# Retention and a routed two-layer network on one core: slots decoded in 16 bits, and what the first gather waits for

## The chip, the core and the metric

The kernel runs on one core of a Trainium2 chip. A core has TensorE (PE; its weight loads have a row of their own, PEld), VectorE (DVE), ScalarE (ACT) and GpSimd (POOL), each with an instruction stream of its own, and queues for DMA: here SyncE's queue writes and loads with plain DMAs, and GpSimd's queue issues the indirect ones (gathers and scatters by row numbers). The metric is device time in microseconds (us) of one execution.

## The reference, cut to what matters

```python
def _attn_ref(q, k, v):                      # (4, 8, 768, 64): batch, heads, steps, width
    for t in range(S):
        state = gamma * state + k_t outer v_t      # gamma differs by head
        y[:, :, t] = scale * (q_t @ state)

def _moe_ref(x, w_gate, w1, w2):             # x: (3072, 512), 8 experts, w1 512 x 1024, w2 1024 x 512
    cap = N // E                             # 384 tokens for each expert
    order = np.argsort(-(x @ w_gate).flatten())
    for idx in order:                        # greedy: the highest (token, expert) pair first
        tok, e = idx // E, idx % E
        if assigned[tok] >= 0 or counts[e] >= cap: continue
        assigned[tok] = e; counts[e] += 1
    for e in range(E):
        out[assigned == e] = np.maximum(x[assigned == e] @ w1[e], 0) @ w2[e]
```

The retention is computed in chunks of 128 steps, and its rows, transposed to one row for each token, are the x of the second part. All are float32; the kernel makes the large products of the network from high and low halves (three matmuls for one).

## The kernel before, in words

**First part (to about 92 us).** 24 units (4 batches by 6 chunks of 128 steps) run through TensorE; VectorE masks the scores, ScalarE copies out. For the rows of x, 17 units are turned on VectorE in 32 by 32 blocks (`block_rows`) and written by the SyncE queue to a DRAM tile `xs`. The last 7 units are turned on TensorE (`row_part`, four transposes for each unit, two to a half), copied by ScalarE to a tile `xr` (`row_out`, a pool of `ROWBUFS` buffers) and written to `xs`. Beside this the gate's logits L are made, and a search for the threshold of the first expert begins.

**Search and decode (`search(n)`, n = 0 to 7 in the order in which experts fill).** The tokens are laid out as 128 partitions by 24 columns. A threshold is found in two counts on TensorE (`count_pairs`), then `Wq` marks the 384 chosen tokens. Two matmuls give each of them its rank; `s0` is 32 plus the rank, or 0. The decode then makes a list of token numbers by slot: `high_slots` splits s0 into `low` (five bits) and `hi`, compares hi with the numbers 0 to 11 (`A`), multiplies by the partition number and by the column number (`V`); `low_slots` compares low with 0 to 31 (`ob`, two tiles); `places` multiplies ob and V on TensorE, six matmuls of 4 columns each; `tokens_of_slots` sums this by four selector matmuls and two VectorE instructions to `idx`. All these small VectorE instructions are called through one helper and stand as L154 in the profile. `bad` collects checks (a group of chosen tokens that isn't 384, and the like); if it is set at the end, a slow exact path (`settle`, after the `If`) runs instead. All the small TensorE results of the search share one PSUM buffer, `psm`.

**The change of part.** The first search is run by hand: `STEPS` says how many halves of rows are turned after each of its steps, and `FILL` how many idle matmuls (`hot<-zer`, 512 columns) TensorE does after the second threshold and after the ranks. The first weights `wraw` are gathered as soon as the expert's code is known (`fetch_w`, L952), then three gathers of x by `idx` (`fetch_x`, L985), then 23 idle matmuls (`HOT`) are run, and the gathered rows `xg` are turned on TensorE (`pt`, L998), copied by ScalarE (`xh`, L1003, behind the first two quarters of the weight split `w1h`, L971) and multiplied (`by_thirds`, L1027).

**Network (to 402 us).** For each expert `mm1` (L1048, `ph`) and `mm2` (L1070, `py`) run on TensorE, with ReLU and splits on ScalarE and VectorE. A planner with rough costs puts the instructions of later searches, weight splits, turns of x and gathers between the matmuls; the order is fixed when the kernel is built.

Of the kernel before, what the change touches and what calls it, by code (L numbers as in the profile page):

```python
# [52 lines left out]
SEND = 10  # L53
STEPS = 7, 1, 2
HOT = 23
WAIT = 3
THIRDS = 2
FILL = (2, 7)
READY0 = 0
# [5 lines left out]
def tile_retention_moe(ctx: ExitStack, tc: tile.TileContext, qkv, wg, w1, w2,  # L65
# [47 lines left out]
    def constants():  # L113
        for t, x in [(onesb, 1.0), (un, 1.0)] + [(t, 0.0) for t in (zer512, Sc, Wq, bad, *sgs)]:
            nc.gpsimd.memset(t, x)
        nc.gpsimd.affine_select(ub, onesb, pattern=[[1, 128]], compare_op=OP.is_gt, fill=0.0, base=0,
                                channel_multiplier=-1)
        nc.gpsimd.affine_select(ident, onesb, pattern=[[1, 128]], compare_op=OP.is_equal, fill=0.0, base=0,
                                channel_multiplier=-1)
        nc.gpsimd.iota(iot, pattern=[[1, 64]], base=0, channel_multiplier=0, allow_small_or_imprecise_dtypes=True)  # L120

    def selectors():
        nc.vector.tensor_reduce(quad, ident.rearrange("p (q r) -> p q r", q=4), axis=AX.X, op=OP.max)
        yield
        nc.vector.tensor_reduce(rowq, ident.rearrange("p (q r) -> p r q", q=4), axis=AX.X, op=OP.max)
        for q in range(4):
            yield
            nc.vector.tensor_scalar(selq[:, q], rowq[:, None, :].to_broadcast([128, 4, 32]), quad[:, q:q + 1], None,
                                    op0=OP.mult)
# [228 lines left out]
    def scores(us):  # L358

        c = units[us[0]][1]  # L360
        for u in us:
            if u == B + 1:
                gate(0)
            k_, q_ = LD[u][:, 0], LD[u][:, 1]
            sc = [bank() for _ in range(2)]
            for pr in range(HP):
                for s in range(2):
                    r, w = slice(64 * s, 64 * s + 64), slice(pr * C, pr * C + C)
                    nc.tensor.matmul(sc[s][:, pr, :], k_[r, w], q_[r, w], start=True, stop=True)  # L369
            am = rw.tile([128, 2, HP, C], F32, name="am", bufs=4)  # L370
            for s in range(2):
                masked.append(nc.vector.tensor_tensor(am[:, s], sc[s], dm[:, s], op=OP.mult))  # L372
            qs = ks = None
            if c:
                qs = rw.tile([128, HP, C], F32, name="qs", bufs=4)
                nc.gpsimd.tensor_tensor(qs, q_.rearrange("p (a b) -> p a b", a=HP), qtb, op=OP.mult)
# [60 lines left out]
    def row_part(pr_, i, d0, d1):  # L437
        b, c = units[i]
        for d in range(d0, d1):
            nc.tensor.transpose(pr_[:, 128 * d:128 * d + 128], YS[b, c][:, d, :], ident)  # L440

    def row_out(pr_, i):
# [8 lines left out]
        t0 = (b * NC + c) * 128  # L451
        nc.sync.dma_start(xs[t0:t0 + 128, :], xr)

# [14 lines left out]
    def send(b, c0, x):  # L468

        xv = xs.rearrange("(b n k) (g x) -> b g k n x", b=B, k=32, g=4)  # L470
        for g in range(4):
            nc.sync.dma_start(xv[b, g ^ 2 * (b % 2), :, 4 * c0:4 * c0 + x.shape[1]], x[32 * g:32 * g + 32])

# [7 lines left out]

    written = []

# [198 lines left out]
    def high_slots(s0, o, n, eng=None):  # L682

        hi = sw.tile([128, COLS], I32, name="hi")
        ve.tensor_scalar(hi, s0, 5, None, op0=OP.arith_shift_right)
        low = sw.tile([128, COLS], I32, name="low")
        ve.tensor_scalar(low, s0, 31, None, op0=OP.bitwise_and)
        A = sw.tile([128, COLS, NB], BF, name="A")
        tt(A, bc(hi, NB), cb(iot[:, o:o + NB], NB), OP.is_equal)
        V = sw.tile([128, COLS, 2, NB], BF, name="V")  # L690
        if eng is None:
            ve.tensor_scalar(V[:, :, 0], A, c_("pcol"), None, op0=OP.mult)
        else:
            eng.activation(V[:, :, 0], A, AF.Copy, scale=c_("pcol"))
        tt(V[:, :, 1], A, bc(tokc, NB), OP.mult)
        return V, low

    def low_slots(low):

        ob = []  # L700
        for c0, c1 in ((0, OBS), (OBS, COLS)):
            ob.append(sw.tile([128, c1 - c0, 32], BF, name=f"ob{c0}"))
            tt(ob[-1], bc(low[:, c0:c1], 32), cb(iot[:, 0:32], 32, c1 - c0), OP.is_equal)
        return ob
# [8 lines left out]
    def places(V, ob, eng=None):  # L713
        pl = ps_small([128, 4, 2 * NB])
        for k in range(COLS // 4):
            c = 4 * k
            o = ob[c // OBS][:, c % OBS:c % OBS + 4]
            te.matmul(flat(pl), flat(o), V[:, c:c + 4].rearrange("p c a n -> p (c a n)"), start=(k == 0),
                      stop=(k == COLS // 4 - 1))
        pls = sw.tile([128, 4, 2 * NB], BF, name="pls")  # L720
# [32 lines left out]
    def search(n):  # L753
# [62 lines left out]
        te.matmul(rk, onesb, Sc[:, 0:COLS + 1], start=False, stop=True)  # L816
        s0 = sw.tile([128, COLS], I32, name="s0")
        ve.scalar_tensor_tensor(s0, rk[:, 0:COLS], 32.0, Wq[:, 0:COLS], op0=OP.add, op1=OP.mult)
        if not last:
            ve.scalar_tensor_tensor(bad, rk[:, COLS:], float(CAP), bad, op0=OP.not_equal, op1=OP.max)  # L820
        if n == 0:
# [33 lines left out]
    def settle(n):  # L855
# [511 lines left out]
```

## Time and profile before

| | |
|---|---|
| runs shown | 404.22, 405.19, 406.41 us (median 405.19) |
| profiled execution | 404.51 us; span of its instructions 402.8 us; granted clock of TensorE 0.997 |
| busy over the span | PE 388.0 us (96%), PEld 337.8 (84%), DVE 274.6 (68%), ACT 156.6 (39%), POOL 147.0 (36%) |
| chain that ended last | PE 61%, DVE 16%, issue 14%, POOL 3%, ACT 2%, DMA 2% |
| DMA | 77.50 MB, mean 192 GB/s |

A row of the chain names the work that the end waited for at that moment. The names are those of the program's tiles without numbers: `V<-A,tokc` writes V from A and tokc. "Idle before" is the time in which the engine did nothing ahead of an instruction, with what ended it behind the arrow; "issue" means that the profile shows nothing that it waited for.

### The profile page before, as it was taken

How to read it: one execution, taken by the hardware profiler on the slowest of the kernel's cores; microseconds unless marked ns; L12 is line 12 of the kernel's file. 1: busy time of each engine (PE TensorE's matmuls, PEld its weight loads, DVE VectorE, ACT ScalarE, POOL GpSimd, SP SyncE). 2: the span in 40 equal slices, each digit the busy share in tenths (PEclk: the TensorE clock that was granted, in tenths of full speed). 3: DMA queues.
4: the chain of work that ended last, by engine and by line, in shares of the span. 5: the costliest groups of instructions: out<-in, count | busy, mean ns of one | idle time of the engine just before them, and what ended most of it. 6: DMA issues, size and time to landing. Idle time of an engine off the chain costs nothing.

```text
span 402.8 us, 8473 instructions
## 1 busy us (share of the span) xinstructions
PE 388.0 (96%) x3457; PEld 337.8 (84%) x3459; DVE 274.6 (68%) x640; ACT 156.6 (39%) x285; POOL 147.0 (36%) x163
## 2 busy tenths in 40 slices
PE   8999999997999999999989999999999999999993
PEld 5998999973798889879868987898799889889982
DVE  5359779878899489859848894897688157156300
ACT  1422434342571264157216524343454165157210
POOL 5488783202611620441261341352255138021011
PEclk9999999999999999999999999999999999999998
DMA  7999998887643762382384383266147316710001
GB/s 284 421 416 421 404 324 247 204 224 244 213 175 104 206 253 55 127 302 105 106 251 192 132 282 137 66 231 253 54 156 244 148 46 181 323 54 26 2 26 60
DMA packets 22825, 77.50 MB, mean 192 GB/s; under 512 B 2678, under 2 KB 11640, under 8 KB 16122
## 3 DMA queue, kind: packets, MB, share of 16 engines
q0 software_dynamic: 8448, 46.14, 32.7%
q1 hardware_dynamic: 14330, 30.74, 21.5%
q8 instruction: 29, 0.48, 0.5%
q14 instruction: 18, 0.14, 0.1%
HBM read 64.29 MB, written 12.58 MB: 191 GB/s over the span
## 4 chain that ended last, share of the span: by engine, by line
PE 61%; DVE 16%; issue 14%; POOL 3%; ACT 2%; DMA 2%; another core or an unknown queue 1%; SPq 0%; POOLq 0%; ACTq 0%; DVEq 0%
PE py L1070 24%; PE ph L1048 20%; PE yp L414 4%; PE sc L369 4%; DVE am L372 3%; PE pt L998 2%; PE psm L154 2%; DVE w1l L154 2%; DMA ld<-qkv 2%; PE TP L429 1%; DVE cmp L154 1%; POOL out L1082 1%; PE sc L501 1%; PE yp L399 1%; PE py L711 1%
## 5 line engine op out<-in xcount | busy, mean ns | idle before, releaser
L1048 PE MATMUL ph<-xh,w1h 128*128 128x384 f32 x248 | 81.9, 343 | 0.1
L1048 PE MATMUL ph<-xlo,w1h 128*128 128x384 f32 x256 | 81.7, 335 | 0.2 <-DVE xlo L154 0.2
L1048 PE MATMUL ph<-xh,w1l 128*128 128x384 f32 x256 | 81.5, 335 | 0.0
L1070 PE MATMUL py<-w2h,hh 128*128 128x512 f32 x192 | 78.4, 408 | 0.0
L1070 PE MATMUL py<-w2l,hh 128*128 128x512 f32 x192 | 75.2, 392 | 0.0
L1070 PE MATMUL py<-w2h,hl 128*128 128x512 f32 x192 | 75.1, 391 | 0.0
L1082 POOL DMA_INDIRECT out<-yo,oix x24 | 28.0, 1165 | 115.2 <-ACT yo L1080 103.7
L952 POOL DMA_INDIRECT wraw<-w,wix x32 | 38.8, 1213 | 60.5 <-DVE un L154 46.9
L1053 ACT ACTIVATE hh<-ph 128x384 fp32r<-128x384 f32 x64 | 31.4, 490 | 61.7 <-PE ph L1048 57.4
L154 DVE TENSOR_TENSOR w1l<-wraw,w1h 128x1024 fp32r<-128x1024 f32 (+1 forms) x36 | 39.3, 1102 | 15.5 <-ACT w1h L971 15.3
L1048 PEld LDWEIGHTS ph<-xlo,w1h 128*128 128x128 f32 x256 | 47.7, 188 | 0.5 <-DVE xlo L154 0.5
L1048 PEld LDWEIGHTS ph<-xh,w1h 128*128 128x128 f32 x248 | 46.4, 188 | 1.6 <-DVE hl L154 0.6
L1048 PEld LDWEIGHTS ph<-xh,w1l 128*128 128x128 f32 x256 | 47.7, 188 | 0.0
L154 DVE SCALAR_TENSOR_TENSOR hl<-ph,hh 128x384 fp32r<-128x384 f32 x64 | 34.5, 553 | 16.0 <-ACT hh L1053 15.4
L985 POOL DMA_INDIRECT xg<-xs,idx x24 | 29.0, 1209 | 42.6 <-issue 27.7
L1070 PEld LDWEIGHTS py<-w2h,hl 128*128 128x128 f32 x192 | 36.1, 188 | 7.8
L372 DVE TENSOR_TENSOR am<-sc,dm 128x512 f32<-128x512 f32 x48 | 30.0, 681 | 17.5 <-PE sc L369 17.5
L1070 PEld LDWEIGHTS py<-w2l,hh 128*128 128x128 f32 x192 | 36.2, 188 | 6.5 <-DVE w2l L154 0.7
L1070 PEld LDWEIGHTS py<-w2h,hh 128*128 128x128 f32 x192 | 36.1, 188 | 5.8
L154 DVE TENSOR_TENSOR w2l<-wraw,w2h 128x1024 fp32r<-128x1024 f32 x32 | 38.6, 1219 | 2.3 <-ACT w2h L971 1.6
L971 ACT ACTIVATE w1h<-wraw 128x1024 fp32r<-128x1024 f32 (+1 forms) x36 | 33.7, 958 | 7.8 <-issue 6.7
L1080 ACT ACTIVATE yo<-py 128x512 f32<-128x512 f32 x23 | 13.8, 598 | 58.6 <-PE py L1070 43.4
(178 smaller groups left out, 544.8 us busy)
## 6 DMA issues: line engine op xcount, KB each, us to landing
ld<-qkv SPq DMA_DIRECT2D x20, 1024.0 KB, 12.2
xs<-x SPq DMA_DIRECT2D x32, 128.0 KB, 3.0
ld<-qkv SPq DMA_DIRECT2D x4, 768.0 KB, 5.4
xs<-xr SPq DMA_DIRECT2D x7, 256.0 KB, 2.1
wraw<-w,wix POOLq DMA_INDIRECT x32
xg<-xs,idx POOLq DMA_INDIRECT x24
out<-yo,oix POOLq DMA_INDIRECT x24
xs<-x SPq DMA_DIRECT2D x4, 64.0 KB, 1.8
```

What stands on the lines that cost most here:

```text
L154: return f(o, *a, **k)
L369: nc.tensor.matmul(sc[s][:, pr, :], k_[r, w], q_[r, w], start=True, stop=True)
L372: masked.append(nc.vector.tensor_tensor(am[:, s], sc[s], dm[:, s], op=OP.mult))
L414: nc.tensor.matmul(yp[o:o + 64, pr, :], values(u)[:, 2 * pr + s, :], st[u][0][:, s, pr, :], start=(not c and pr == 0), stop=(pr == HP - 1) ...
L952: nc.gpsimd.indirect_dma_start(out=t, out_offset=None, in_=w1v if nm == "w1" else w2v, in_offset=bass.IndirectOffsetOnAxis(ap=wix[:, hf:hf ...
L971: nc.scalar.activation(p[0], p[2], AF.Copy)
L985: nc.gpsimd.indirect_dma_start(out=t, out_offset=None, in_=xs, in_offset=bass.IndirectOffsetOnAxis(ap=found[n][0][:, j:j + 1], axis=0))
L1048: nc.tensor.matmul(ph, a[:, o:o + 128], x_[:, d], start=(k == 0 and not begun), stop=(k == len(prods) - 1), skip_group_check=begun)
L1053: nc.scalar.activation(hh[:, f], ph, AF.Relu)
L1070: nc.tensor.matmul(py, h_[:, f, t], a[:, o:o + DM], start=(k == 0), stop=(k == 23))
L1080: nc.scalar.activation(yo, py, AF.Copy)
L1082: sct = nc.gpsimd.indirect_dma_start(out=out, out_offset=bass.IndirectOffsetOnAxis(ap=oix[:, j:j + 1], axis=0), in_=yo, in_offset=None, bo ...
```

## The change

It has four parts.

1. **Decode in 16 bits.** `s0`, `low` and `hi` become int16, and the number tables they are compared with become bfloat16 tables made at the start on GpSimd (`iolow`, 128 elements, `iohigh`, 312). `low` is taken first and `hi` is `s0 - low`, so hi now waits for low. A, V and ob are laid out with the tokens' columns innermost. So V is now read by the slot matmuls with a step of 24 elements, and the selectors `selq` of the last sum are built from another table (`four`, one VectorE reduction more).
2. **Checks behind the token numbers (first search only).** The check of the ranks goes from in front of `low` to behind `ob`; the other two (three instructions) go behind `idx`. In the later searches the checks stay where they were.
3. **First gather.** A GpSimd memset (`early`) waits for everything that wrote or read `xs` and the buffers (the list `gone`); the first gather of x behind it waits for VectorE alone.
4. **Rows in one go.** `STEPS` 7, 1, 2 becomes 9, 1, 0; `FILL` 2, 7 becomes 5, 7; `ROWBUFS` 4 becomes 5.

```diff
-ROWBUFS = 4
+ROWBUFS = 5
-STEPS = 7, 1, 2
+STEPS = 9, 1, 0
-FILL = (2, 7)
+FILL = (5, 7)
+    iolow = sw.tile([128, 32, 4], BF, name="iolow")
+    iohigh = sw.tile([128, NB + 1, COLS], BF, name="iohigh")
...
+        for t, k in ((iolow, 1), (iohigh, 32)):
+            nc.gpsimd.iota(t, pattern=[[k, t.shape[1]], [0, t.shape[2]]], base=0, channel_multiplier=0,
+                           allow_small_or_imprecise_dtypes=True)
...
+        nc.vector.tensor_reduce(four, ident.rearrange("p (j r) -> p r j", r=4), axis=AX.X, op=OP.max)
...
-        hi = sw.tile([128, COLS], I32, name="hi")
-        ve.tensor_scalar(hi, s0, 5, None, op0=OP.arith_shift_right)
-        low = sw.tile([128, COLS], I32, name="low")
+        low = sw.tile([128, COLS], I16, name="low")
         ve.tensor_scalar(low, s0, 31, None, op0=OP.bitwise_and)
-        A = sw.tile([128, COLS, NB], BF, name="A")
-        tt(A, bc(hi, NB), cb(iot[:, o:o + NB], NB), OP.is_equal)
-        V = sw.tile([128, COLS, 2, NB], BF, name="V")
+        hi = sw.tile([128, COLS], I16, name="hi")
+        tt(hi, s0, low, OP.subtract)
+        A = sw.tile([128, NB, COLS], BF, name="A")
+        tt(A, hi[:, None, :].to_broadcast([128, NB, COLS]), iohigh[:, o:o + NB], OP.is_equal)
+        V = sw.tile([128, 2, NB, COLS], BF, name="V")
...
-            ob.append(sw.tile([128, c1 - c0, 32], BF, name=f"ob{c0}"))
-            tt(ob[-1], bc(low[:, c0:c1], 32), cb(iot[:, 0:32], 32, c1 - c0), OP.is_equal)
+            k = (c1 - c0) // 4
+            ob.append(sw.tile([128, k, 32, 4], BF, name=f"ob{c0}"))
+            tt(ob[-1], low[:, c0:c1].rearrange("p (k r) -> p k r", r=4)[:, :, None, :].to_broadcast([128, k, 32, 4]),
+               iolow[:, None].to_broadcast([128, k, 32, 4]), OP.is_equal)
...
-            o = ob[c // OBS][:, c % OBS:c % OBS + 4]
-            te.matmul(flat(pl), flat(o), V[:, c:c + 4].rearrange("p c a n -> p (c a n)"), start=(k == 0),
-                      stop=(k == COLS // 4 - 1))
+            o = ob[c // OBS][:, c % OBS // 4]
+            te.matmul(flat(pl), flat(o), V[:, :, :, c:c + 4].rearrange("p a n c -> p c (a n)"),
+                      start=(k == 0), stop=(k == COLS // 4 - 1))
...
-        if not last:
+        def full_rows():
             ve.scalar_tensor_tensor(bad, rk[:, COLS:], float(CAP), bad, op0=OP.not_equal, op1=OP.max)
+        if n and not last:
+            full_rows()
...
         ob = low_slots(low)
-        if not last:
-            ve.scalar_tensor_tensor(bad, both, code, bad, op0=OP.not_equal, op1=OP.max)
-            alone(oh, unf if n else None)
+        if n == 0:
+            full_rows()
+        elif not last:
+            one_left()
...
         idx = tokens_of_slots(pls)
+        if n == 0:
+            one_left()
...
+    early = nc.gpsimd.memset(spacer, 0.0)
+    for o_ in gone:
+        tc.add_manual_dep(early.ins, o_.ins.name, ...)
     side.finish(0)
```

How the order of instructions changes, at three places. The line numbers differ by the lines that the change adds (L154 is now L162, L952 is L978, L985 is L1011).

VectorE, the first decode, before (from the ranks to the copy of the slot sums):

```order
L154 SCALAR_TENSOR_TENSOR s_1679<-psm,Wq 128x24
L154 SCALAR_TENSOR_TENSOR bad<-psm,bad 128x1
L154 TENSOR_SCALAR hi<-s_1679 128x24
L154 TENSOR_SCALAR low<-s_1679 128x24
L154 TENSOR_TENSOR A<-hi,iot 128x288
L154 TENSOR_TENSOR V<-A,tokc 128x24x12
L154 TENSOR_TENSOR ob_1699<-low,iot 128x384
L154 TENSOR_TENSOR ob_1701<-low,iot 128x384
L154 SCALAR_TENSOR_TENSOR bad<-both,code,bad 128x1
L154 TENSOR_REDUCE et<-oh 128x1
L154 SCALAR_TENSOR_TENSOR bad<-et,bad 128x1
L154 CAST pls<-psm 128x96
```

The same stretch now:

```order
L162 SCALAR_TENSOR_TENSOR s_1689<-psm,Wq 128x24
L162 TENSOR_SCALAR low<-s_1689 128x24
L162 TENSOR_TENSOR hi<-s_1689,low 128x24
L162 TENSOR_TENSOR A<-hi,iohigh 128x288
L162 TENSOR_TENSOR V<-A,tokc 128x288
L162 TENSOR_TENSOR ob_1708<-low,iolow 128x384
L162 TENSOR_TENSOR ob_1710<-low,iolow 128x384
L162 SCALAR_TENSOR_TENSOR bad<-psm,bad 128x1
L162 CAST pls<-psm 128x96
L162 TENSOR_TENSOR own<-psm,quad 128x24
L162 TENSOR_REDUCE idx<-own 128x3
L162 SCALAR_TENSOR_TENSOR bad<-both,code,bad 128x1
```

The check that reads the ranks' PSUM (`bad<-psm,bad`) went from the second place to behind ob; the other three checks are now behind idx; hi stands behind low.

GpSimd, from the first gather of weights on, with what each instruction waits for, before:

```order
L952 DMA wraw_95<-w,wix 128x2048 [waits DVE_49]
L985 DMA xg<-xs,idx 128x512 [waits DMAHW3_49,DMAHW2_49,DMAHW4_49,DMAHW1_49,DMAHW5_49,DMAHW0_49,DMAHW6_49,DVE_49,DMAHW7_49,PE_49,Pool_49]
L985 DMA xg<-xs,idx 128x512 x2
L952 DMA wraw<-w,wix 128x2048
L1156 COPY spacer<-xh 1x1 [waits Activation_49]
```

And now:

```order
L978 DMA wraw_98<-w,wix 128x2048 [waits DVE_49]
L1152 MEMSET spacer 1x1 [waits DMAHW3_49,DMAHW4_49,DMAHW2_49,DMAHW5_49,DMAHW1_49,DMAHW6_49,DMAHW0_49,DMAHW7_49,PE_49,Pool_49]
L1011 DMA xg<-xs,idx 128x512 [waits DVE_49]
L1011 DMA xg<-xs,idx 128x512 x2
L978 DMA wraw<-w,wix 128x2048
L1186 COPY spacer<-xh 1x1 [waits Activation_49,Pool_49]
```

Of the eleven waits of the first gather of x, ten went to the memset ahead of it, and VectorE's stayed.

TensorE, the first slot matmuls, with their waits, before:

```order
L711 MATMUL py<-zer,onesb 128x512
L154 LDWEIGHTS ob_1699 [waits PE_49,DVE_49]
L154 MATMUL psm<-V,ob_1699 128x96 [waits Activation_49]
L154 LDWEIGHTS ob_1699
L154 MATMUL psm<-V,ob_1699 128x96
L154 LDWEIGHTS ob_1699
L154 MATMUL psm<-V,ob_1699 128x96
L154 LDWEIGHTS ob_1701 [waits DVE_49]
L154 MATMUL psm<-V,ob_1701 128x96
```

And now:

```order
L726 MATMUL py<-zer,onesb 128x512
L162 LDWEIGHTS ob_1708 [waits PE_49,DVE_49]
L162 MATMUL psm<-V,ob_1708 128x96 [waits Activation_49]
L162 LDWEIGHTS ob_1708
L162 MATMUL psm<-V,ob_1708 128x96
L162 LDWEIGHTS ob_1708
L162 MATMUL psm<-V,ob_1708 128x96
L162 LDWEIGHTS ob_1710
L162 MATMUL psm<-V,ob_1710 128x96
```

Before, the second tile of ob had a wait for VectorE of its own. Now the first weight load's wait covers it: the sums go to the one psm buffer, which the check behind the second ob has to have read.

## Rows read from the trace of the kernel before

**Rows 1.** Windows. Columns: stretch, length, busy of each engine (instructions), clock, DMA share.
```profile
104.00:357.00 253.00, 250.10 (x1496) 220.09 (x1497) 181.97 (x431) 106.90 (x175) 86.49 (x92) 1.00 0.49 172
```

**Rows 2.** The chain of waits, 86 to 113 us. Columns: start us, us, engine and line.
```profile
95.29 0.94 DVE ob L154 x2
...
97.29 4.99 PE py L711 x23
...
103.44 0.60 ACT xh L1003
```

**Rows 3.** Timeline of VectorE. Columns: start us, us, line, operation, out<-in, shapes, idle.
```profile
93.56 0.13 DVE L154 SCALAR_TENSOR_TENSOR wix<-code,cs 128x2 int32<-128x2 f32 x1
...
93.91 0.18 DVE L154 SCALAR_TENSOR_TENSOR s<-psm,Wq 128x24 int32<-128x24 f32 x1
94.01 0.15 DVE L154 SCALAR_TENSOR_TENSOR bad<-psm,bad 128x1 f32<-128x1 f32 x1
94.13 0.18 DVE L154 TENSOR_SCALAR hi<-s 128x24 int32<-128x24 int32 x1
...
94.34 0.46 DVE L154 TENSOR_TENSOR A<-hi,iot 128x288 bf16<-128x288 int32 x1
94.83 0.46 DVE L154 TENSOR_TENSOR V<-A,tokc 128x288 bf16<-128x288 bf16 x1
95.21 1.02 DVE L154 TENSOR_TENSOR ob<-low,iot 128x384 bf16<-128x384 int32 x2
...
96.74 0.25 DVE L154 CAST pls<-psm 128x96 bf16<-128x96 f32 x1
...
97.54 0.19 DVE L154 TENSOR_REDUCE idx<-own 128x3 int32<-128x24 f32 x1
...
99.68 0.26 DVE L154 TENSOR_TENSOR eqc<-oh,codeo 128x192 bf16<-128x192 bf16 x1
```

**Rows 4.** Timeline of GpSimd, the first gathers.
```profile
93.99 1.16 POOL L952 DMA_INDIRECT wraw<-w,wix  x1 [20.18 <-DVE un L154]
98.58 1.11 POOL L985 DMA_INDIRECT xg<-xs,idx  x1 [3.43 <-DVE lim L154]
```

**Rows 5.** Timeline of ScalarE around the first gathers.
```profile
93.39 0.66 ACT L448 ACTIVATE xr<-py 128x256 f32<-128x256 f32 x2 [0.93 <-PE py L440]
...
102.11 1.15 ACT L971 ACTIVATE w1h<-wraw 128x512 fp32r<-128x512 f32 x2 [6.74 <-issue]
```

**Rows 6.** Timeline of TensorE, the count of pairs.
```profile
91.19 0.31 PE L154 MATMUL psm<-oh,cmp 128*128 128x16 bf16 x6 [0.56 <-DVE cmp L154]
```

**Rows 7.** DMA issues of the page. Columns: out<-in, queue, KB each, median us to landing.
```profile
xs<-xr SPq DMA_DIRECT2D x7, 256.0 KB, 2.1
```

**Rows 8.** Timeline of TensorE, the first rows of x.
```profile
102.70 0.66 PE L998 MATMUL pt<-ident,xg 128*128 128x128 f32 x4 [0.43 <-DMA xg<-xs,idx]
```

**Rows 9.** Timeline of GpSimd at the start.
```profile
3.96 0.40 POOL L120 IOTA iot<- 128x64 f32 x1
6.41 1.04 POOL L379 TENSOR_TENSOR ld<-ld,ktb 128x512 f32<-128x512 f32 x1 [2.06 <-DMA ktb<-ktab]
```

**Rows 10.** The chain of waits over the whole span, two later decodes.
```profile
192.71 0.47 DVE A L154
...
193.86 0.94 DVE ob L154 x2
...
290.60 0.66 DVE V L154 x2
```

**Rows 11.** Timeline of TensorE, the slot matmuls of a later decode.
```profile
163.45 0.43 PE L154 MATMUL psm<-V,ob 128*128 128x96 bf16 x6
```

**Rows 12.** Waits of TensorE, 110 to 357 us. Columns: waiter <- releaser: us, times, longest.
```profile
PE psm L154 <- DVE sg L154: 2.0, 1, 2.0
...
PE ph L1048 <- DVE xlo L154: 0.2, 1, 0.2
```

**Rows 13.** Timeline of ScalarE, a late count.
```profile
210.17 0.17 ACT L220 ACTIVATE ng<-psm 64x8 f32<-64x8 f32 x1 [5.08 <-remote]
```

More of the change, by code (lines that the diff above doesn't have):

```diff
@@ L11 @@
 I32 = mybir.dt.int32
+I16 = mybir.dt.int16
 U32 = mybir.dt.uint32
@@ L102, in tile_retention_moe @@
     quad = sw.tile([128, 4], F32, name="quad")
+    four = sw.tile([128, 4], F32, name="four")
     rowq = sw.tile([128, 32], F32, name="rowq")
@@ L120, in constants @@
         nc.gpsimd.iota(iot, pattern=[[1, 64]], base=0, channel_multiplier=0, allow_small_or_imprecise_dtypes=True)
+        for t, k in ((iolow, 1), (iohigh, 32)):
+            nc.gpsimd.iota(t, pattern=[[k, t.shape[1]], [0, t.shape[2]]], base=0, channel_multiplier=0,
+                           allow_small_or_imprecise_dtypes=True)
     def selectors():
         nc.vector.tensor_reduce(quad, ident.rearrange("p (q r) -> p q r", q=4), axis=AX.X, op=OP.max)
+        nc.vector.tensor_reduce(four, ident.rearrange("p (j r) -> p r j", r=4), axis=AX.X, op=OP.max)
         yield
-        nc.vector.tensor_reduce(rowq, ident.rearrange("p (q r) -> p r q", q=4), axis=AX.X, op=OP.max)
+        nc.vector.tensor_reduce(rowq, ident.rearrange("p (j r) -> p j r", r=4), axis=AX.X, op=OP.max)
         for q in range(4):
             yield
-            nc.vector.tensor_scalar(selq[:, q], rowq[:, None, :].to_broadcast([128, 4, 32]), quad[:, q:q + 1], None,
+            nc.vector.tensor_scalar(selq[:, q], rowq[:, None, :].to_broadcast([128, 4, 32]), four[:, q:q + 1], None,
                                     op0=OP.mult)
@@ L375, in scores @@
                 qs = rw.tile([128, HP, C], F32, name="qs", bufs=4)
-                nc.gpsimd.tensor_tensor(qs, q_.rearrange("p (a b) -> p a b", a=HP), qtb, op=OP.mult)
+                scaled = nc.gpsimd.tensor_tensor(qs, q_.rearrange("p (a b) -> p a b", a=HP), qtb, op=OP.mult)
+                if u == nu - 1:
+                    gone.append(scaled)
             if c < NC - 1:
@@ L439, in row_part @@
         for d in range(d0, d1):
-            nc.tensor.transpose(pr_[:, 128 * d:128 * d + 128], YS[b, c][:, d, :], ident)
+            turned = nc.tensor.transpose(pr_[:, 128 * d:128 * d + 128], YS[b, c][:, d, :], ident)
+        if i == len(units) - 1:
+            gone.append(turned)
     def row_out(pr_, i):
@@ L451, in row_out @@
         t0 = (b * NC + c) * 128
-        nc.sync.dma_start(xs[t0:t0 + 128, :], xr)
+        gone.append(nc.sync.dma_start(xs[t0:t0 + 128, :], xr))
     x2, x1 = {}, {}
@@ L471, in send @@
         for g in range(4):
-            nc.sync.dma_start(xv[b, g ^ 2 * (b % 2), :, 4 * c0:4 * c0 + x.shape[1]], x[32 * g:32 * g + 32])
+            gone.append(nc.sync.dma_start(xv[b, g ^ 2 * (b % 2), :, 4 * c0:4 * c0 + x.shape[1]],
+                                          x[32 * g:32 * g + 32]))
     def send_two():
@@ L480, in send_one @@
         send(*units[i], x1[i].rearrange("p t d r -> p t (d r)"))
-    written = []
+    written, gone = [], []
     def rows_left(tile_of):
@@ L682, in high_slots @@
     def high_slots(s0, o, n, eng=None):
-        hi = sw.tile([128, COLS], I32, name="hi")
-        ve.tensor_scalar(hi, s0, 5, None, op0=OP.arith_shift_right)
-        low = sw.tile([128, COLS], I32, name="low")
+        low = sw.tile([128, COLS], I16, name="low")
         ve.tensor_scalar(low, s0, 31, None, op0=OP.bitwise_and)
-        A = sw.tile([128, COLS, NB], BF, name="A")
-        tt(A, bc(hi, NB), cb(iot[:, o:o + NB], NB), OP.is_equal)
-        V = sw.tile([128, COLS, 2, NB], BF, name="V")
+        hi = sw.tile([128, COLS], I16, name="hi")
[3 more added lines that the diff above has]
+        V = sw.tile([128, 2, NB, COLS], BF, name="V")
         if eng is None:
-            ve.tensor_scalar(V[:, :, 0], A, c_("pcol"), None, op0=OP.mult)
+            ve.tensor_scalar(V[:, 0], A, c_("pcol"), None, op0=OP.mult)
         else:
-            eng.activation(V[:, :, 0], A, AF.Copy, scale=c_("pcol"))
-        tt(V[:, :, 1], A, bc(tokc, NB), OP.mult)
+            eng.activation(V[:, 0], A, AF.Copy, scale=c_("pcol"))
+        tt(V[:, 1], A, tokc[:, None, :].to_broadcast([128, NB, COLS]), OP.mult)
         return V, low
@@ L816, in search, with one_left @@
         te.matmul(rk, onesb, Sc[:, 0:COLS + 1], start=False, stop=True)
-        s0 = sw.tile([128, COLS], I32, name="s0")
+        s0 = sw.tile([128, COLS], I16, name="s0")
         ve.scalar_tensor_tensor(s0, rk[:, 0:COLS], 32.0, Wq[:, 0:COLS], op0=OP.add, op1=OP.mult)
-        if not last:
+        def full_rows():
             ve.scalar_tensor_tensor(bad, rk[:, COLS:], float(CAP), bad, op0=OP.not_equal, op1=OP.max)
+        def one_left():
+            ve.scalar_tensor_tensor(bad, both, code, bad, op0=OP.not_equal, op1=OP.max)
+            alone(oh, unf if n else None)
+        if n and not last:
+            full_rows()
         if n == 0:
@@ L921, in settle @@
         tt(s1, s2t[:, 0:COLS], s2t[:, COLS:], OP.add)
-        s0 = sw.tile([128, COLS], I32, name="s0")
+        s0 = sw.tile([128, COLS], I16, name="s0")
         ve.tensor_scalar(s0, s1, -1.0, None, op0=OP.add)
@@ L1125, in tile_retention_moe @@
             next(rows, None)
+    early = nc.gpsimd.memset(spacer, 0.0)
+    for o_ in gone:
+        tc.add_manual_dep(early.ins, o_.ins.name, mybir.DependencyInfo(
+            mybir.DependencyClass.Sync, mybir.DependencyReason.DATA), reason="what the first gather of x waits for")
     side.finish(0)
```

## The prediction

> **What bounds the kernel now.** I read the shares first, then the windows, then the chain of waits between the two parts, and last the timeline of each engine there. From 104 to 357 us TensorE is busy for 250.1 of 253.0 us at full clock [rows 1]. In the network, then, a shorter VectorE instruction is worth only what TensorE waited for it, and a longer TensorE instruction costs all of itself. Between the parts it is otherwise. There the chain runs through VectorE's decode (ob), its sums, 23 idle matmuls, and then through the first turned rows to ScalarE's copy xh, which ends at 104.04 and from where TensorE is full [rows 2]. The reader is to see that this stretch is latency: each step waits for the one before. Whatever makes xh earlier moves all that follows, since gathers, splits and searches of the network are released by each other and not by a clock. So the change is worth G, by which xh comes earlier, and H, what the seven later decodes gain or lose.
>
> **The decode, n = 0.** A VectorE instruction that makes 288 bfloat16 elements from a 32-bit or one-element-step operand takes 0.46, a pair of 384 takes 1.02 with 0.08 of overlap, 0.55 each; 96 elements cost 0.09 to 0.10, one nanosecond an element. eqc has 16-bit operands alone, with the columns contiguous, and makes 192 in 0.26 [rows 3]. At the slope of the others 192 would take 0.36, so eqc runs at half the price of an element, and the fixed part is 0.16. In that form A and V take 0.31 each and ob 0.36 each. No row has int16 operands; the bounds are this and no gain at all. I take the halves, because int16 is as wide as eqc's operands.
>
> From s0's end (94.09) on [rows 3]: low 94.13 to 94.30 at hi's price; hi waits for low now, 94.32 to 94.49 (before, hi and low stood side by side and A began at 94.34, so this costs 0.18); A 94.52 to 94.83; V to 95.16; ob 95.08 to 95.70 (before 96.23). Two things follow behind ob. The check of the ranks, 0.15 [rows 3], ends at about 95.82, and by the order all six slot matmuls wait for it, since it reads the PSUM buffer that they overwrite; before, three of them ran under the second ob. Six take 0.43 in a later decode [rows 11], so the sums are there at 96.29 where before the copy pls began at 96.74. pls starts at 96.31: 0.43 earlier. (Before, three checks stood in front of pls and held it to 96.74 where the matmuls would have let it go at about 96.62; that 0.12 is in the sum.) idx ends at 97.30 and not 97.73 [rows 3]. The three checks behind idx keep the next search where it was, 0.1 us earlier at most; its results aren't asked for on this path.
>
> **The gather.** Before, it starts at 98.58, 0.85 behind idx's end. The weights' gather, which waits for VectorE alone, starts at 93.99, 0.30 behind its index (93.69) [rows 3, 4]. With one wait left I take 0.30: the gather starts at 97.60, 0.98 earlier. The bounds are 0.30 and 0.85. What hides the ten waits now is the memset ahead; behind it on GpSimd stand the three gathers of x and the second half of the weights, so it must be through before 97.3. The last row copy ends at 94.05 [rows 5], and a write lands 2.1 later [rows 7], at 96.2: already before it would just do. With the rows in one go the last halves are turned where now unit 22's are, behind the count; its copies take 0.66 from about 91.86, so the write lands at 94.7, 2.6 ahead of idx. Turning 18 and not 14 blocks in front of the count puts its first six matmuls back by about 0.25; the second six wait for cmp until 91.19 anyway [rows 6], so this costs nothing. The fifth xr buffer takes away a wait of 0.28 for a write. Five idle matmuls at 0.217 each (4.99 for 23 [rows 2]) fill 1.09 us between the threshold and the ranks, where the two and the last turns stood; they are through at 93.2, Wq is ready at 93.4.
>
> **What is late next.** The 23 idle matmuls start with the selector sums, 0.43 earlier, and end at 101.85. The rows came 4.12 behind their gather's start (98.58 to 102.70 [rows 4, 8]), which makes 101.72. So the turn starts at 101.87 and G is at most 0.83. But ScalarE copies the first two quarters of the weights ahead of xh, from 102.11 to 103.26 [rows 5], for weights whose gather isn't moved. If they land no sooner, xh can start at 103.26 and not 103.44: G = 0.18. They share the DMA engines with the last rows' write, which is now over about 1.5 us earlier, when their gather has just been issued. I take G = 0.65 between these ends, nearer to the upper one, since the lag of the rows and of the weights has lost its neighbour.
>
> **The later decodes, H.** Each is shorter by 0.15 (A), 0.15 (V), 0.39 (ob), less 0.1 for hi: about 0.6 on VectorE, seven times. TensorE waited for VectorE four times in 247 us, 2.0 to 0.2 us each; the first is a count that ScalarE copied late (at 210.17, for no reason that the profile has) [rows 12, 13], and the other three make 0.8. Decodes stand on the chain at 192.7 and 290.6 [rows 10]. So H lies between 0 and 1.2, two decodes; I take 0.5, most of the 0.8.
>
> **At nothing.** GpSimd's two new tables are 440 elements; 64 take 0.40, so 0.8 to 2.8 us, in a gap of 2.06 before 6.41 [rows 9]; what is over delays a scaling that is asked for four us later. One more reduction of 0.24 in the first part: 0 to 0.24, I take 0.
>
> **Sum.** G 0.65 and H 0.5 make 1.15 off the profiled 404.51: 403.4. That execution lies 0.7 under the median of the runs shown, 405.19; the forecast is for the median, 405.19 - 1.15 = **404.0 us**. Its own range is 403.2 (G 0.83, H 1.2) to 405.0 (G 0.18, H 0).
>
> **Rivals.**
> *V read in steps (slower).* The slot matmuls now read V with a step of 24 elements. Contiguous, an idle matmul's column costs 0.42 ns (0.217 for 512 [rows 2]), 96 of them 0.041. No row has a stepped operand on TensorE. The dearest column near by is that of float32 turns: 0.66 for four [rows 8], about 0.125 for 128 columns, 2.3 times as much. At that price 42 later matmuls cost 0.053 more each, 2.2 us in a part that has no slack [rows 1], and six in the first decode 0.3: 404.0 + 2.5 = 406.5. It outweighs the gain from 1.6 times the plain column on. For it: TensorE is full. Against: six take 0.43 as they are [rows 11], 0.07 each with their weight loads, so a dearer column may stay hidden behind a load.
> The Trainium skill, "SBUF — State Buffer", section "Door 1: The DMA port swizzle (why [64,N] ≈ [32,N])", speaks against this change: it says that reads run at full rate only while neighbours fall into one 16-byte line, eight bfloat16, and V's step is 48 bytes. It gives no price; no row here shows one. By it this rival holds, without it the forecast.
> *The weights hold ScalarE.* xh waits for the weight split, which starts at 102.11 as before: G 0.18, H 0.5, 404.5. For it: the gather of the weights isn't moved.
> *The 16-bit forms aren't faster.* Then low in front of hi costs 0.18, ob ends at 96.42, idx at 98.0; the gather still gains 0.25, G 0.1, H 0: 405.1.
> *The late count.* The wait of 2.0 us at 208.6 [rows 12] isn't tied to anything the change touches; it may vanish (402.0) or a second one come (406.0).
>
> **Chances.** Forecast 0.50, stepped V 0.17 (a third of it past 407.2), weights 0.13, no faster forms 0.08, late count 0.12, half each way. The range that holds eight in ten is 402.2 to 406.4: it takes in the late count's lower case nearly and the stepped V's price, and leaves out its dearer third. 0.5% is 2.0 us, about what a measurement of this kernel can tell from no change. Under 403.16: the upper end of the forecast with the runs' own spread of 1 us, and half the late count, 0.27. Over 407.2: 0.11. Between: 0.62.
>
> **What would show it.** A and V at 0.31 and ob at 0.36 (if 0.46 and 0.55, the third rival); the slot matmuls of the first decode all behind the check; the gather of x at about 97.6, 0.3 behind idx; the memset on GpSimd done before 96; xh at 102.6 to 102.8. The slot matmuls' six in a later decode at 0.43 (0.7 or more would be the first rival). If xh is earlier by 0.6 and the end isn't, something in the network has given it back, and my view that all moves along is wrong.

## The result, and the profile after

The changed kernel takes 409.09 us (median of 10 runs, 406.89 to 410.49), the kernel before 406.00 us beside it (10 runs, 404.05 to 407.43): a ratio of 1.0083, 95% interval 1.0059 to 1.0107. It is slower by 3.4 us by the ratio (3.1 by the medians), where 1.15 less, 404.0, was forecast with a range of 402.2 to 406.4.

The page of the changed kernel, its span and the shares:

```profile
span 406.3 us, 8485 instructions
PE 393.7 (97%) x3460; PEld 342.5 (84%) x3462; DVE 271.1 (67%) x641; ACT 156.5 (39%) x285; POOL 146.4 (36%) x166
```

The span grew by 3.5 us (402.8 before), VectorE's busy time fell by 3.5 and TensorE's grew by 5.7 (388.0 before). So it is not a wait that came in: TensorE is busy for longer, with 3460 instructions on the page where it had 3457. From 104 to 357 us it is as full as it was [rows 1]; the window's row:

```profile
104.00:357.00 253.00, 250.68 (x1476) 220.24 (x1476) 177.89 (x431) 106.04 (x172) 84.91 (x91) 1.00 0.49 170
```

The timeline of TensorE, first decode and a later one (start us, us, line, operation, out<-in, shapes, idle), says what grew:

```profile
95.89 1.17 PE L162 MATMUL psm<-V,ob 128*128 128x96 bf16 x6 [0.46 <-DVE bad L162]
...
97.51 5.12 PE L726 MATMUL py<-zer,onesb 128*128 128x512 bf16 x23
...
102.47 0.60 PE L1024 MATMUL pt<-ident,xg 128*128 128x128 f32 x4
...
163.73 1.17 PE L162 MATMUL psm<-V,ob 128*128 128x96 bf16 x6
```

Six slot matmuls took 0.43 us in a later decode [rows 11] and take 1.17, in the first decode and in the later one alike: 0.74 more, and eight decodes make 5.9, about TensorE's growth of 5.7. The timeline of VectorE in the first decode, which answers to [rows 3]:

```profile
93.95 0.18 DVE L162 SCALAR_TENSOR_TENSOR s<-psm,Wq 128x24 int16<-128x24 f32 x1
94.17 0.17 DVE L162 TENSOR_SCALAR low<-s 128x24 int16<-128x24 int16 x1
94.37 0.17 DVE L162 TENSOR_TENSOR hi<-s,low 128x24 int16<-128x24 int16 x1
94.58 0.31 DVE L162 TENSOR_TENSOR A<-hi,iohigh 128x288 bf16<-128x288 int16 x1
94.92 0.31 DVE L162 TENSOR_TENSOR V<-A,tokc 128x288 bf16<-128x288 bf16 x1
95.15 0.62 DVE L162 TENSOR_TENSOR ob<-low,iolow 128x384 bf16<-128x384 int16 x2
95.68 0.15 DVE L162 SCALAR_TENSOR_TENSOR bad<-psm,bad 128x1 f32<-128x1 f32 x1
97.10 0.26 DVE L162 CAST pls<-psm 128x96 bf16<-128x96 f32 x1 [1.27 <-PE psm L162]
...
97.92 0.18 DVE L162 TENSOR_REDUCE idx<-own 128x3 int32<-128x24 f32 x1
```

VectorE is through 0.4 us earlier (bad ends at 95.83, ob before at 96.23) and then stands 1.27 us for TensorE. GpSimd [rows 4] and ScalarE [rows 2, 5], one after the other:

```profile
95.19 0.09 POOL L1152 MEMSET spacer<- 1x1 f32 x1
98.38 0.94 POOL L1011 DMA_INDIRECT xg<-xs,idx  x1 [3.10 <-DVE idx L162]
```
```profile
99.88 1.15 ACT L997 ACTIVATE w1h<-wraw 128x512 fp32r<-128x512 f32 x2 [4.43 <-DMA wraw<-w,wix]
103.16 0.60 ACT L1029 ACTIVATE xh<-pt 128x512 fp32r<-128x512 f32 x1 [2.13 <-issue]
```

The memset stands right behind the gather of the weights and is through at 95.28. The gather of x starts 0.28 behind the end of idx (0.85 before), as the change means it to, yet at 98.38 and not at 97.6; xh comes 0.28 earlier than before. The late count is there as it was [rows 12], in the waits of TensorE from 110 to 357 us:

```profile
PE psm L162 <- DVE sg L162: 1.9, 1, 1.9
```

Executions start their decode at slightly different times, so below xh is counted from the start of s in the same execution: 103.44 - 93.91 = 9.53 before, 103.16 - 93.95 = 9.21 after.

### The profile page after: what moved, and what is told of

Same layout as the page of the kernel before. It is cut to its first block, busy times and chain, and to the rows that moved or that the text cites. A ratio compares the mean times of both kernels' runs of the same rounds, so it can differ in the third digit from the quotient of the medians.

```text
span 406.3 us, 8485 instructions
## 1 busy us (share of the span) xinstructions
PE 393.7 (97%) x3460; PEld 342.5 (84%) x3462; DVE 271.1 (67%) x641; ACT 156.5 (39%) x285; POOL 146.4 (36%) x166
## 4 chain that ended last, share of the span: by engine, by line
PE 70%; issue 14%; DVE 11%; POOL 3%; ACT 2%; POOLq 0%; DVEq 0%; ACTq 0%; another core or an unknown queue 0%
PE py L1096 25%; PE ph L1074 24%; PE yp L424 4%; PE sc L377 4%; PE psm L162 4%; DVE am L380 3%; PE pt L1024 2%; PE TP L439 1%; DVE cmp L162 1%; POOL out L1108 1%; PE sc L514 1%; PE yp L409 1%; DVE x L477 1%; POOL wraw L978 1%; DVE w1l L162 1%
## 5 line engine op out<-in xcount | busy, mean ns | idle before, releaser
L978 POOL DMA_INDIRECT wraw<-w,wix x32 | 37.5, 1172 | 60.8 <-DVE un L162 46.9
L162 DVE TENSOR_TENSOR w1l<-wraw,w1h 128x1024 fp32r<-128x1024 f32 (+1 forms) x36 | 39.3, 1102 | 15.3 <-ACT w1h L997 15.3
L162 DVE SCALAR_TENSOR_TENSOR hl<-ph,hh 128x384 fp32r<-128x384 f32 x64 | 34.8, 553 | 19.5 <-ACT hh L1079 19.0
L1011 POOL DMA_INDIRECT xg<-xs,idx x24 | 28.8, 1201 | 46.0 <-issue 33.6
L162 DVE TENSOR_TENSOR w2l<-wraw,w2h 128x1024 fp32r<-128x1024 f32 x32 | 38.6, 1218 | 2.4 <-ACT w2h L997 2.4
```

What stands on the lines that cost most here:

```text
L162: return f(o, *a, **k)
L978: nc.gpsimd.indirect_dma_start(out=t, out_offset=None, in_=w1v if nm == "w1" else w2v, in_offset=bass.IndirectOffsetOnAxis(ap=wix[:, hf:hf ...
L1011: nc.gpsimd.indirect_dma_start(out=t, out_offset=None, in_=xs, in_offset=bass.IndirectOffsetOnAxis(ap=found[n][0][:, j:j + 1], axis=0))
```

## The experiments

Theory 1: V read in steps of 48 bytes costs TensorE four times the plain price per column, and that is the whole loss. Theory 2: the loss is VectorE's order (checks moved, low ahead of hi). Theory 3: the early memset, the fill and the fifth row buffer.

**v_in_runs.** The four columns of a matmul become the innermost dimension of the operand; the eviction (the copy of the sums from PSUM to `pls`) turns the result back.

```diff
-        pl = ps_small([128, 4, 2 * NB])
+        pl = ps_small([128, 2 * NB, 4])
-            ... V[:, :, :, c:c + 4].rearrange("p a n c -> p c (a n)")
+            ... V[:, :, :, c:c + 4].rearrange("p a n c -> p (a n) c")
...
+        to = pls.rearrange("p c x -> p x c")
...
-            nc.scalar.activation(pls, pl, AF.Copy)
+            nc.scalar.activation(to, pl, AF.Copy)
...
-            eng.tensor_copy(pls, pl)
+            eng.tensor_copy(to, pl)
```

> The changed kernel, but the slot matmuls read V in runs of four neighbouring columns (8 bytes) instead of single columns 48 bytes apart, and the eviction of pls turns the result back. Theory 1 (TensorE reads single columns 48 bytes apart at about four times the price of neighbours: 1.17 us for six against 0.43 to 0.46): six slot matmuls take 0.45 us again in all eight decodes, xh of the first decode starts near 102.5 us instead of 103.16, the seven later decodes give back 0.6 us each, and the time is 0.994 to 0.998 of the kernel before. Theory 2 (the loss comes from VectorE's order: checks moved behind, low before hi, the next search later): the six may get shorter, but the decodes still start later and later, and the time stays at 1.006 to 1.010. Theory 3 (the new wait of the early memset, the larger fill, the fifth row buffer): also 1.006 to 1.010, with the loss in the stretch up to 104 us.

400.82 us against 402.33: 0.9953 (0.9940 to 0.9965). Rows of its timeline, first decode and the slot matmuls of a later one:

```profile
96.21 0.18 DVE L162 SCALAR_TENSOR_TENSOR s<-psm,Wq 128x24 int16<-128x24 f32 x1
...
98.16 0.43 PE L162 MATMUL psm<-V,ob 128*128 128x96 bf16 x6 [0.46 <-DVE bad L162]
...
98.63 0.57 DVE L162 CAST pls<-psm 128x96 bf16<-128x96 f32 x1 [0.53 <-PE psm L162]
...
105.05 0.60 ACT L1030 ACTIVATE xh<-pt 128x512 fp32r<-128x512 f32 x1 [1.60 <-issue]
...
164.71 0.43 PE L162 MATMUL psm<-V,ob 128*128 128x96 bf16 x6
```

The six are at 0.43 again, xh stands at 8.84 behind s, though the turned eviction takes 0.57 and not 0.26 us, and the loss has become a gain, with the checks, the memset and the fill untouched. Theories 2 and 3 fall as the cause of the loss.

**no_16bit.** The changed kernel without its first part (old `high_slots`, `low_slots`, `places` and tables).

```diff
-        A = sw.tile([128, NB, COLS], BF, name="A")
-        tt(A, hi[:, None, :].to_broadcast([128, NB, COLS]), iohigh[:, o:o + NB], OP.is_equal)
+        A = sw.tile([128, COLS, NB], BF, name="A")
+        tt(A, bc(hi, NB), cb(iot[:, o:o + NB], NB), OP.is_equal)
...
```

> The changed kernel without its first part: slots are decoded as in the kernel before (32-bit hi and low, columns outermost, V neighbouring), and only the moved checks, the early memset with its waits, the fill of 5 and the rows turned in one go stay. Theory 1 (all of the loss is in the stepped read of V): 0.996 to 1.001 of the kernel before, xh of the first decode 0.3 to 0.6 us earlier, six slot matmuls 0.43 us. Theories 2 and 3 (checks and order, or memset and fill): most of the loss stays, 1.005 to 1.010.

401.78 us against the same 402.33: 0.9983 (0.9969 to 0.9998). xh comes 102.82 - 93.85 = 8.97 behind s, and the gather of x 4.20 behind it:

```profile
93.85 0.18 DVE L155 SCALAR_TENSOR_TENSOR s<-psm,Wq 128x24 int32<-128x24 f32 x1
...
102.82 0.60 ACT L1020 ACTIVATE xh<-pt 128x512 fp32r<-128x512 f32 x1 [1.87 <-issue]
```

So the other parts by themselves are worth 0.56 us to xh. Between this kernel and v_in_runs lies the 16-bit decode alone: 0.96 us by the medians, of which xh has 0.13. By the intervals of the two ratios that difference is uncertain by some 0.8 us.

**before_stepped.** The kernel before with the stepped read alone.

```diff
-            ... V[:, c:c + 4].rearrange("p c a n -> p (c a n)")
+            ... V[:, c:c + 4].rearrange("p c a n -> p n (c a)")
...
```

> The kernel before, with one thing changed: its slot matmuls read V in steps of 12 elements (24 bytes), since the moving operand is taken with the block of 32 slots outermost and the token column innermost; the eviction of pls turns the result back. Nothing is moved on VectorE before the slot matmuls. Theory 1 (a stepped read costs TensorE up to four times): six slot matmuls take 1.0 to 1.2 us instead of 0.43, and the time is 1.008 to 1.013 of the kernel before, all in the decodes. If 24 bytes are cheaper than 48, six take between 0.43 and 1.0 and the loss is in proportion. Theories 2 and 3: no change, 0.998 to 1.002.

407.95 us against 402.33: 1.0154 (1.0128 to 1.0180), 6.2 us more by the ratio, 5.6 by the medians, a little over the 1.013 expected at most; TensorE's busy time on its page is 394.1 us. One row of its timeline:

```profile
164.58 1.20 PE L154 MATMUL psm<-V,ob 128*128 128x96 bf16 x6
```

The full price is there at 24 bytes, 1.20 for six, and it brings the loss into a kernel in which nothing else of the change is made. Eight decodes at 0.77 make 6.2. (Its eviction turns the result too, 0.61 us where it was 0.25; no_turn below bounds what that costs.)

**steps.** What a column costs by how far apart the columns lie: 24 matmuls of 96 columns for each case, back to back.

> A measurement apart, that computes nothing of the reference: 24 matmuls of 96 columns for each way of reading the moving operand, with steps of 1 to 32 bf16 elements, runs of 2, 4 and 8 neighbours at pitches of 8 to 24 elements, and fp32 in steps of 1 to 12. Theory 1: neighbours take about 0.042 us a matmul at the full clock, runs of four about as much, single columns 24 elements apart about 0.168 us; where between 1 and 24 elements the price rises is open: by the bytes of the step, in two or more levels. Theories 2 and 3: all bf16 steps 0.042 to 0.1 us, by which 1.17 us for six in the changed kernel would have to be a wait and not the read.

Windows of this kernel, one for each case; behind the length stand the busy times and counts of TensorE, weight loads, VectorE and GpSimd, then the granted clock. In order: bfloat16 in steps of 1, 2, 4, 6, 8, 12 and 24 elements, runs of four at a pitch of 24 and of 8 elements, float32 in steps of 1, 2 and 4.

```profile
14.14:15.16 1.02, 1.02 (x26) 1.02 (x25) 0.69 (x1) 0.00 (x0) 1.00 0.00 0
15.16:16.22 1.06, 1.06 (x28) 1.06 (x26) 0.00 (x0) 0.00 (x0) 1.00 0.06 15
16.22:18.32 2.10, 2.10 (x28) 2.10 (x26) 0.00 (x0) 0.00 (x0) 1.00 0.00 0
18.32:21.44 3.12, 3.12 (x27) 2.80 (x25) 0.00 (x0) 0.00 (x0) 1.00 0.00 0
21.44:25.57 4.13, 4.13 (x26) 2.93 (x24) 0.00 (x0) 0.00 (x0) 0.72 0.00 0
25.57:29.68 4.11, 4.11 (x26) 3.03 (x24) 0.00 (x0) 0.00 (x0) 0.50 0.00 0
33.87:37.95 4.08, 4.08 (x26) 3.00 (x24) 0.00 (x0) 0.00 (x0) 0.50 0.00 0
43.97:45.87 1.90, 1.90 (x27) 1.90 (x25) 0.00 (x0) 0.00 (x0) 0.50 0.00 0
47.49:48.52 1.03, 1.03 (x28) 1.03 (x26) 0.00 (x0) 0.00 (x0) 1.00 0.06 16
49.59:54.98 5.39, 5.39 (x52) 5.39 (x50) 0.00 (x0) 0.00 (x0) 1.00 0.00 0
54.98:60.35 5.37, 5.37 (x51) 5.37 (x49) 0.00 (x0) 0.00 (x0) 1.00 0.01 3
60.35:68.65 8.30, 8.30 (x50) 8.30 (x49) 0.00 (x0) 0.00 (x0) 1.00 0.00 0
```

A window begins with the first of a case's 24 matmuls and ends with the start of the next case; counts over 24 are matmuls that reach across an edge. A 24th of each window is a bfloat16 matmul: 0.043 us in steps of 2 and 4 bytes, 0.088 at 8 bytes, 0.130 at 12, 0.172 at 16, and from there 0.171 and 0.170 at 24 and 48 bytes (by windows left out here 0.175 at 32 and 0.164 at 64). This is a staircase by pieces of 16 bytes: 96 columns at 8 bytes touch 48 of them, at 12 bytes 72, from 16 bytes on 96, and each costs 1.8 ns, while a column alone costs 0.44 at the full clock. The dearer of the two sets the time: at 8 bytes the pieces make 0.086 and the columns 0.042, and 0.088 is taken, not the sum. Runs of four at a pitch of 16 bytes touch 24 pieces and take 0.043 at full clock. float32 fits (48 matmuls recorded, so two for each): its 0.112 a matmul stays at 8 bytes, 48 pieces, and is 0.173 at 16 bytes, 96 pieces. The Trainium skill, "SBUF — State Buffer", section "Door 1: The DMA port swizzle (why [64,N] ≈ [32,N])", has the 16-byte line, and these windows agree on its size; it also says that two hits in a line are enough for the full rate and that eight bfloat16 may be stepped for free, and here two hits in a line (8 bytes) already cost bfloat16 twice the plain price, while for float32 they are enough.

**no_turn, no_turn_early, only_16bit, no_turn_early_hot19.** In no_turn pls stays as it comes, and its reader steps:

```diff
-        pls = sw.tile([128, 4, 2 * NB], BF, name="pls")
+        pls = sw.tile([128, 2 * NB, 4], BF, name="pls")
-            te.matmul(ip, flat(selq[:, q]), pls[:, q], ...)
+            te.matmul(ip, flat(selq[:, q]), pls[:, :, q], ...)
```

The second moves `full_rows()` of the first decode back behind s0; the third is the kernel before with the 16-bit decode, runs of four and unturned pls; the fourth is the second with `HOT = 19`.

> The changed kernel with V read in runs of four, as in v_in_runs, but the eviction of pls no longer turns the result: pls is stored as it comes, and the four small matmuls behind it read it in steps of four elements (8 bytes). By theory 1 and by the 0.088 us that 96 columns in steps of 8 bytes took in the measurement apart (0.0425 for neighbours), these four matmuls of 24 columns cost some 0.01 us more each, and the eviction falls from 0.61 to 0.25 us: 0.3 us less in each of eight decodes, 2.4 us less than v_in_runs, 0.988 to 0.991 of the kernel before. Theory 1b (the eviction is hidden beside TensorE's other work in the seven later decodes): only the first decode gains, 0.3 us, 0.994 to 0.996.

> As no_turn, and the first decode's check of the full rows stands right behind s again, as in the kernel before. If the check in front of the slot matmuls costs the first decode time (it is queued behind the second ob on VectorE, and TensorE started 0.46 us late behind it in the changed kernel), three of the six slot matmuls run beside the second ob, and the first gather of x starts 0.05 to 0.3 us earlier against s than in no_turn; the check itself puts 0.15 us in front of low and hi, so it may as well be 0.1 us later. In the time: 0.9990 to 1.0005 of no_turn. If the moved check carries a gain of its own, 0.3 us later.

> The kernel before with the first part of the change alone (16-bit operands, columns innermost), V read in runs of four and pls not turned; checks, early memset, fill and row turning as in the kernel before. The three edits on VectorE shorten a decode by 0.15 us (A), 0.15 (V) and 0.40 (two ob): theory 1 expects 0.3 to 0.6 us less for each later decode, 2 to 4.5 us in all, 0.989 to 0.995 of the kernel before. If the slots lie beside TensorE's other work in the later decodes (theory 1c), only the first gains, 0.5 us: 0.998 to 1.000.

> As no_turn_early, with 19 instead of 23 matmuls of zeros between the first slots and the first transposes (0.22 us each). In the changed kernel these ended at 102.63 us by their row, 0.16 us behind the start of the transposes that follow them. If they hold the transposes, those start up to 0.5 us earlier, as soon as the gathered rows are in; if the gather's landing holds them, nothing moves but the idle time: within 0.0005 of no_turn_early, or slower if the granted clock falls below 1.00 in the stretch behind.

Against 403.43 us: 401.62 (0.9959, 0.9944 to 0.9975), 401.48 (0.9957, 0.9928 to 0.9985), 401.58 (0.9958, 0.9940 to 0.9976) and 401.92 (0.9961, 0.9945 to 0.9978). None differs from another, or from v_in_runs (0.9953), beyond these intervals. So the 2.4 us that I expected of the eviction aren't there, and theory 1b's range holds: in the trace of v_in_runs TensorE waits for pls once, 0.7 us in the first decode, and never in the seven later ones. only_16bit lands between its two brackets. It also does as well as the kernels with the whole change: once the slots are decoded in 16 bits, the moved checks, the memset and the rows in one go add nothing to the time that these runs could measure, though by themselves (no_16bit) they were worth some 0.6 us. From s the gather starts at 3.70, 3.50, 4.18 and 3.50 us (so the check of the ranks, moved behind ob, costs the gather 0.20), and yet the first turn starts at 7.92, 7.95, 7.97 and 7.96. In only_16bit:

```profile
94.26 0.18 DVE L162 SCALAR_TENSOR_TENSOR s<-psm,Wq 128x24 int16<-128x24 f32 x1
...
98.44 1.11 POOL L995 DMA_INDIRECT xg<-xs,idx  x1 [2.94 <-DVE lim L162]
...
100.78 1.15 ACT L981 ACTIVATE w1h<-wraw 128x512 fp32r<-128x512 f32 x2 [5.01 <-DMA wraw<-w,wix]
...
102.23 0.66 PE L1008 MATMUL pt<-ident,xg 128*128 128x128 f32 x4
```

In the fourth kernel, where s starts at 94.74, the gather and the turn show what holds it, since no fill is in the way there:

```profile
98.24 0.94 POOL L1009 DMA_INDIRECT xg<-xs,idx  x1 [2.17 <-DVE idx L162]
...
102.70 0.65 PE L1022 MATMUL pt<-ident,xg 128*128 128x128 f32 x4 [1.08 <-DMA xg<-xs,idx]
```

**x_before_weights.** The fourth kernel with the first gather of weights behind those of x.

```diff
-            fetch_w("w1", 0, 0, wix.bitcast(U32), raw0)
+            pass
...
     for j in range(KT):
         fetch_x(0, j)
+    fetch_w("w1", 0, 0, found[0][1], raw0)
     fetch_w("w1", 1, 0, found[0][1])
```

> As no_turn_early_hot19, with the first gather of weights (1 MB) issued behind the three gathers of x instead of 4 us ahead of them. There the first x was gathered 3.50 us behind the start of s and its transposes began only 7.96 us behind s, waiting for the DMA, as in the three kernels whose gather started 3.70 to 4.18 us behind s. If the 1 MB of weights in front of it holds the x back, the transposes start 0.5 to 1.5 us earlier against s (6.5 to 7.4 us), while the first product starts later, behind the weights, so that the time is some 1 to 3 us longer. If the landing takes its 4.1 to 4.5 us by itself, the transposes start 7.6 to 8.0 us behind s, as they do.

```profile
95.58 0.18 DVE L162 SCALAR_TENSOR_TENSOR s<-psm,Wq 128x24 int16<-128x24 f32 x1
...
99.10 1.17 POOL L1009 DMA_INDIRECT xg<-xs,idx  x1 [2.38 <-DVE idx L162]
...
102.78 0.66 PE L1022 MATMUL pt<-ident,xg 128*128 128x128 f32 x4 [0.32 <-DMA xg<-xs,idx]
...
111.04 1.12 PE L1051 MATMUL ph<-xh,w1h 128*128 128x128 f32 x4 [6.96 <-ACT xh L1027]
```

The turn starts 7.20 behind s, and 3.68 behind its gather instead of 4.46. So, by this one run, the 1 MB of weights ahead of it holds x back by some 0.8 us. That fits only_16bit, whose gather starts 0.7 us later than the fourth kernel's and loses nothing by it. Weights that come last cost more than that: the first product waits 6.96 us, xh comes 14.8 us behind s instead of 8.7, and behind that wait the granted clock is 0.50 (1.2 GHz) from 112 to 118 us. The one run took 415.92 us, some 10 over the kernel before on that chip (406.05) and 12 over v_in_runs_again (403.78), where 1 to 3 were expected.

**changed_again, v_in_runs_again, before_again.**

> The changed kernel once more, on the same chip as v_in_runs_again. Theory 1: 1.006 to 1.010 of the kernel before.

> v_in_runs once more, beside the changed kernel on the same chip. Theory 1: 0.994 to 0.998 of the kernel before, and 4.5 to 6 us less than changed_again, nearly all of it TensorE's busy time in eight times six slot matmuls (0.74 us each time).

> The kernel before, for its profile on this chip. In the profiles of before and after, TensorE stood 1.9 to 2.0 us idle near 209 us behind a late count of one decode; in the other kernels' profiles it stood 0.0 to 0.5 us there. If that stall belongs to the execution and not to the program, this profile may lack it, and its span is then 1.5 to 2 us shorter; if it belongs to the kernel before, it is there again, at the same decode.

409.28 and 403.78 us against 406.05: 1.0093 (1.0066 to 1.0120) and 0.9946 (0.9922 to 0.9971). The one edit of the operand's order is worth 5.5 us. From s, xh comes at 9.45 in before_again, 9.21 in changed_again and 8.78 in v_in_runs_again. The late count is in all three (in before_again: `PE psm L154 <- DVE sg L154: 2.0, 1, 2.0`), while on two other chips v_in_runs, no_16bit and no_turn stood 0.0 to 0.5 us there. v_in_runs has it on one chip and not on another, so in these profiles, one for each kernel and chip, it goes with the chip and not with the kernel; why ScalarE comes late there stays open.

## Why the prediction was wrong

- **VectorE's forms: right.** A and V take 0.31 as forecast, two ob 0.62 for 0.62, hi waits for low, by which A begins 0.63 behind the start of s and not 0.43: 0.20 (0.18 forecast), and bad ends at 95.83 (95.82).
- **The wait of the gather: right.** 0.28 behind idx, with 0.30 taken. The memset is through at 95.28, before 96 as forecast.
- **The failing step: the six slot matmuls at 0.43.** The forecast took over the price of a V read in order and put the cost of the stepped read at nothing. They take 1.17, so pls starts at 97.10 and not at 96.31, and everything up to the gather (98.38 for 97.60) is late by the same 0.8. In the later decodes the same 0.74 falls on a TensorE without slack, where, the prediction said, a longer instruction costs all of itself: seven times 0.74 is 5.2.
- **The rival had the mechanism and not the price.** "V read in steps" took the price from a float32 turn, 2.3 times a plain column, as "the dearest column near by": 0.053 us a matmul. before_stepped and steps show 0.127 (0.170 less 0.043), four times. By that price the forecast's own sum gives 404.0 + 42 × 0.127 + 0.74 = 410.1, which is 4.9 over the 405.19 that it started from, where 3.4 (2.4 to 4.3) were measured: right in direction and 1.5 too much. Of this 0.4 is at xh, which that sum has 0.09 later and the runs have 0.32 earlier. The measured time lies in the dearer third of this rival, which the range left out. The reason I gave against it, that a dearer column may hide behind a weight load, is refuted by v_in_runs: the weight loads are the same, and the six take 0.43 or 1.17. An operand of a kind that no row had deserved a bound from how far it departs from what the rows have, and that bound had no reason to end at a float32 turn.
- **G, 0.65: close once the read is mended, in part by luck.** xh comes 0.69 earlier against s in v_in_runs, with the stepped read 0.32. But v_in_runs pays 0.3 us for its turned eviction, which the forecast doesn't have; in no_turn, which pays neither, xh comes 8.67 behind s, 0.86 earlier, a little over the upper end of 0.83. The rival that the weights hold ScalarE is wrong as put: in the changed kernel w1h starts at 99.88 and is through at 101.03, two us ahead of xh. It starts 2.3 us sooner against s than before (5.93 and not 8.20), and the forecast's reason, the rows' write that is over earlier, may be part of it; but in only_16bit, whose last rows are copied as late as before, w1h starts 6.52 behind s, so what held it before stays open. And the weights do hold the rows of x, on the DMA side, as x_before_weights shows.
- **H, 0.5: within its bounds, and the size is not settled.** v_in_runs is 0.96 us under no_16bit, 0.13 of it at xh, and the 0.83 left lies within the bounds of 0 to 1.2, but the difference is uncertain by about as much as it is large.
- **The late count** neither vanished nor doubled.

The whole, from the runs: 0.32 off at xh, 0.83 off and 5.2 on in the seven later decodes make 4.0 us more. Measured are 3.4, with an interval of 2.4 to 4.3, so these parts are enough.

The version that beats both is v_in_runs: 0.9953 and 0.9946 of the kernel before, with the whole change and one operand in another order. only_16bit, the kernel before with the mended 16-bit decode alone, does as well (0.9958).

## What to carry over

A layout that suits VectorE (columns innermost) is paid for by whoever reads it next: before turning an operand, work out how many 16-byte pieces each matmul will touch, at 1.8 ns each against 0.44 ns a column at the full clock (steps, bfloat16). Where the operand has free dimensions, put neighbours innermost in the read and let the output carry the order; turning it back cost the first gather 0.3 us and the whole time nothing that these runs could measure. A rival with a known mechanism and an unknown price needs a range that is open upwards, and above all where it falls on the one engine without slack.

## What the runs showed of the hardware

The stepped read does not follow TensorE's clock. In the measurement apart the granted clock was 1.00 (2.4 GHz) while the steps were 2 to 12 bytes, fell during the 16-byte steps (0.72 over that window) and was 0.50 (1.2 GHz) at 24 and 48 bytes; the matmul took 0.172, 0.171 and 0.170 all the same. Within the window of the 16-byte steps the matmuls start 0.170 to 0.174 us apart on both sides of the fall. Runs of four at 0.50 took 0.079, 1.8 times the 0.043 at full clock. TensorE was busy throughout before the fall, in steps of 12 and 16 bytes, and the clock was 1.00 again at 47.49 us, behind runs of four and eight. In the changed kernel no such fall shows (clock 1.00 from 104 to 357 us).

The clock did dip in two executions behind the idle time of the late count, from 212 to 218 us: in changed_again, and in v_in_runs_again likewise (0.77), not in before_again (1.00). The row of changed_again:

```profile
212.00:218.00 6.00, 5.24 (x22) 4.25 (x21) 4.90 (x9) 2.92 (x5) 0.39 (x1) 0.72 0.92 373
```
